# Sharing SBUF-operand work between VectorE and GpSimd by the order of the instructions, in attention followed by two feed-forward layers

## The chip, the cores and the metric

The kernel runs on one core of one Trainium2 chip. The metric is device time in microseconds (us) of one execution. TensorE is called PE here (PEld its weight loads), VectorE DVE, ScalarE ACT, GpSimd POOL, and SyncE, whose queue issues the transfers, SP.

## What is computed

Attention with 4 batches, 8 heads, 576 tokens and a head size of 64, in which only scores within `tau` of their row's maximum count. Its output, 2304 tokens of 512 numbers, goes through two feed-forward layers with a hidden size of 2048. The first uses a leaky ReLU with a slope for each hidden unit, the second x * sigmoid(x), which is Silu.

```python
scores = scale * np.matmul(q, k.transpose(0, 1, 3, 2))
thresh = np.max(scores, axis=-1, keepdims=True) - tau
scores = np.where(scores >= thresh, scores, -1000000000.0)
attn = np.exp(scores - np.max(scores, axis=-1, keepdims=True))
attn = attn / (np.sum(attn, axis=-1, keepdims=True) + 1e-09)
x = heads_side_by_side(np.matmul(attn, v))
h = x @ w_in;   g = np.maximum(h, 0.0) + alpha * np.minimum(h, 0.0);   x = g @ w_out
h = x @ w_in2;  g = h * (1.0 / (1.0 + np.exp(-h)));                    out = g @ w_out2
```

(The last three lines are put together from three functions.) The weights come as 64-bit numbers in memory; the kernel converts them itself.

## The kernel before

**Attention** works on 16 pairs of heads, each with 9 units of up to 128 rows of scores. For each of the 144 units PE multiplies into PSUM; DVE scales, copies to SBUF and takes the extreme (`maxi`, L481, `x<-s,nsc`: it reads PSUM); ACT takes the exponential (`expo`, L494); and DVE compares with the threshold and multiplies (`mask`, L507, `e<-x,m,e`: both operands in SBUF). Then come transposes, the products with v, and `evac` (L594, `X<-pv,px`) into the tiles X0, X1 and X2, each with 768 tokens.

**Each layer** goes in 12 passes: 4 groups of 512 hidden units by 3 pieces p of 768 tokens. A pass forms 7 products of the Strassen kind (`PORD`: 1, 7, 6, 2, 5, 3, 4), each of 2 x 6 matmuls, since every operand stands as a high part and a rest, and three of the four cross products are taken. `piece` makes the token side of a product in an `xs` tile: subtractions for T2, T3 and T4 into `ta` and `tb` (L342), ACT's high part (`one`, L223), and the rest `x - high` (L346), which POOL does for every other product and DVE for the others. In a layer's first group the pieces are made; they are stored, and read back for the later groups. Product sums go through `c<-c,su`, `su<-s,su` and `s<-s,su` (L854, L858, L864: one operand in PSUM) to `act`, which makes the hidden value `r` (L753 and L754 in the first layer; in the second Sigmoid, L757, and a multiplication, L758), its high part and its rest `g` (L760, 192 times). Then PE forms the output blocks y (`yblock`, L775 and L777; 8 a pass in the first layer, 6 in the second), half of them at the end of the pass, half in the next.

**Weights** are converted by `conv`, one 128x512 block at a time: 4 `wi` and 4 `wo` for each group. A block is loaded as `raw`; two ACT steps and five DVE steps (L290, L292, L294, L299 or L301, L302) make a float `cv`, with `cm` and `ce` as scratch; and a high part and a rest are written to the `wi` or `wo` tile (for `wi` after four sums into `cs`, L314). The product `ce<-ce,cm` is done by DVE in attention (L301) and by POOL after it (L299). During attention six blocks (4 `wi`, `WOA` = 2 `wo`) and the pieces of products 1 and 7 are prepared.

**What sets the order.** All of it is issued by two planners that place steps in a model with assumed durations. `plan` (attention) has PE follow the list `ORDER`; on the other engines, of the steps that can start first, the one with the smallest priority number goes, and conversions and pieces have the last. `plan_late` (the layers) takes the step that is due first, counting back from PE's order. Each engine then runs its queue in the order that was planned and waits only for data. Every step is tied to one engine, and both planners treat DVE and POOL as engines that don't touch each other:

```python
t = max(free[e], min(ready[n] for n in able(e)))
n = min((n for n in able(e) if ready[n] <= t), key=lambda n: (ops[n][3], rank[n]))
```

Of the kernel before, what the change touches and what calls it, by code (L numbers as in the profile page):

```python
# [41 lines left out]
XO = 40  # L42
XSB = 5
WIB = 7
WOB = 8
WOA = 2
GB = 12
RSB = 3
VB = 2
RB = 2  # L50
# [37 lines left out]

def plan(ops, order, seq):
    left, ready, out, after = {}, {}, [], {}  # L90
# [5 lines left out]
    free = {e: 0.0 for e in ("PE", "DVE", "ACT", "POOL", "SP")}  # L96
    cand = {e: [] for e in free}
    rank = {n: i for i, n in enumerate(ops)}
    for n in ops:
        if not left[n]:  # L100
            cand[ops[n][0]].append(n)
# [48 lines left out]
def plan_late(ops):  # L150

    n = len(ops)
    after = [[] for _ in range(n)]
# [14 lines left out]
    free = {e: 0.0 for e in ("PE", "DVE", "ACT", "POOL", "SP")}  # L168
    cand = {e: [] for e in free}
    for i, o in enumerate(ops):  # L170
        if o[0] != "PE" and not left[i]:
            cand[o[0]].append(i)
    k, out = 0, []
    while True:
        best = None
        for e in free:
            c = ([pe[k]] if k < len(pe) and not left[pe[k]] else []) if e == "PE" else cand[e]
            if c:
                t = max(free[e], min(ready[i] for i in c))
                if best is None or t < best[0]:  # L180
                    best = (t, e, c)
# [3 lines left out]
        i = min((i for i in c if ready[i] <= t), key=lambda i: (late[i], i))  # L185
        if e == "PE":
            k += 1
        else:
            cand[e].remove(i)
        o = ops[i]  # L190
        free[e] = t + o[1]
        out.append((t, len(out), i))
        for j in after[i]:
            ready[j] = max(ready[j], t + (o[1] if e == ops[j][0] == "PE" else o[2]))
            left[j] -= 1
            if not left[j] and ops[j][0] != "PE":
                cand[ops[j][0]].append(j)
    assert len(out) == n
# [4 lines left out]
def attn_moe_moe(  # L203
# [66 lines left out]
    def conv(kind, n, r, pool):  # L270
# [7 lines left out]
        else:  # L278
# [647 lines left out]
```

## Time and profile before

| | |
|---|---|
| three runs, median | 1086.74 us (1085.68 to 1087.17) |
| the profiled execution, its own time | 1087.49 us |
| its span, first to last instruction | 1085.7 us |
| mean granted TensorE clock | 0.991 of full |
| busy: PE, DVE, ACT, POOL | 96%, 79%, 60%, 12% of the span |

The span leaves out 1.8 us that lie around the instructions. A busy share is a mean over stages with different limits, so the stretches below are read one by one. The duration of an instruction in the records runs from its start to its end, and time in which it stands still after its start is part of it.

### The profile page before, as it was taken

What the parts mean: (1) busy time and instruction counts of PE and PEld (TensorE: products, weight loads), DVE (VectorE), ACT (ScalarE), POOL (GpSimd) and SP (SyncE); (2) the same over time, 40 slices, a digit from 0 to 9 for tenths busy, and PEclk for the clock granted to TensorE, in tenths of its full rate; (3) what the DMA queues carried; (4) which work ended last, traced back from release to release, by engine and by line L of the source; (5) the groups of instructions that cost most, each with busy time, mean ns of one, the idle gap of its engine ahead of it and who ended that gap; (6) DMA issues with size and microseconds to landing.
All of it is one profiled execution on the core that took longest, in us unless ns stands there. A gap on an engine that the chain in (4) does not pass through costs nothing.

```text
span 1085.7 us, 16589 instructions
## 1 busy us (share of the span) xinstructions
PE 1045.5 (96%) x6020; PEld 887.6 (82%) x6021; DVE 856.2 (79%) x1880; ACT 650.6 (60%) x1303; POOL 126.6 (12%) x88
## 2 busy tenths in 40 slices
PE   9999999999778999999999999899999999999998
PEld 5665666566577999999999998887898888889987
DVE  7999999999589887688768787887778588655443
ACT  6889889988556675455545545666565355333320
POOL 0000000000243321001101102233111011000000
PEclk9999999999989999999999999999999999999999
DMA  3223223141354775576765665455676555555632
GB/s 106 89 75 103 84 80 103 53 150 39 145 203 195 244 253 197 185 257 242 238 215 190 213 211 203 155 214 185 232 262 230 196 191 217 174 204 204 228 130 78
DMA packets 43601, 189.30 MB, mean 174 GB/s; under 512 B 5120, under 2 KB 5504, under 8 KB 43520
## 3 DMA queue, kind: packets, MB, share of 16 engines
q1 hardware_dynamic: 43216, 187.97, 49.6%
q8 instruction: 47, 0.77, 0.3%
q10 hardware_dynamic: 304, 0.28, 0.1%
q14 instruction: 34, 0.28, 0.1%
HBM read 150.48 MB, written 37.75 MB: 173 GB/s over the span
## 4 chain that ended last, share of the span: by engine, by line
PE 67%; DVE 23%; issue 5%; POOL 2%; ACT 2%; POOLq 0%; DVEq 0%; ACTq 0%
PE s L359 20%; PE y L777 16%; PE y L775 12%; PE s L467 5%; PE t L541 4%; PE pv L575 4%; PE c L359 3%; DVE x L481 3%; DVE e L507 3%; DVE g L760 3%; POOL ce L299 2%; DVE r L754 2%; DVE r L758 1%; DVE cv L302 1%; DVE cv L292 1%
## 5 line engine op out<-in xcount | busy, mean ns | idle before, releaser
L359 PE MATMUL s<-xs,wi 128*128 128x384 f32 x1728 | 327.2, 341 | 22.2 <-DVE su L858 5.1
L359 PEld LDWEIGHTS s<-xs,wi 128*128 128x128 f32 x1728 | 304.7, 190 | 36.3 <-DVE r L758 7.8
L775 PE MATMUL y<-g,wo 128*128 128x384 f32 x1152 | 209.8, 338 | 10.0 <-ACT g L223 4.1
L775 PEld LDWEIGHTS y<-g,wo 128*128 128x128 f32 x1152 | 201.8, 190 | 14.4 <-DVE X L792 4.8
L777 PE MATMUL y<-wo,g 128*128 128x512 f32 (+1 forms) x876 | 202.0, 389 | 1.3 <-DVE X L792 0.7
L777 PEld LDWEIGHTS y<-wo,g 128*128 128x128 f32 x876 | 163.1, 189 | 34.9 <-DVE X L792 1.2
L223 ACT ACTIVATE su<-s 128x384 f32<-128x384 f32 x144 | 70.3, 489 | 111.6 <-PE s L359 110.7
L299 POOL TENSOR_TENSOR ce<-ce,cm 128x512 f32<-128x512 f32 x58 | 78.5, 1353 | 455.3 <-ACT cm L296 232.9
L223 ACT ACTIVATE g<-r 128x384 fp32r<-128x384 f32 x192 | 97.8, 523 | 36.2 <-DVE r L754 21.1
L481 DVE TENSOR_SCALAR_CACHE_REDUCE x<-s,nsc 128x576 f32<-128x576 f32 x144 | 112.5, 814 | 1.9 <-PE s L467 1.6
L760 DVE TENSOR_TENSOR g<-r,g 128x384 fp32r<-128x384 f32 x192 | 108.5, 584 | 0.0
L467 PE MATMUL s<-raw 64*128 64x288 f32 (+1 forms) x576 | 100.8, 427 | 1.0 <-DVE x L481 1.0
L507 DVE SCALAR_TENSOR_TENSOR e<-x,m,e 128x577 f32<-128x577 f32 x128 | 100.1, 811 | 1.2 <-ACT m L501 1.1
L494 ACT ACTIVATE e<-x,m 128x576 f32<-128x576 f32 x128 | 97.1, 785 | 5.0 <-DVE x L481 4.8
L792 DVE TENSOR_TENSOR X<-y,X 128x384 f32<-128x384 f32 (+1 forms) x108 | 64.5, 598 | 31.4 <-PE y L777 20.8
L467 PEld LDWEIGHTS s<-raw 64*128 64x128 f32 (+1 forms) x576 | 57.0, 186 | 39.2 <-DVE x L481 11.3
L302 DVE TENSOR_TENSOR cv<-cv,ce 128x512 f32<-128x512 f32 x64 | 48.0, 750 | 45.9 <-POOL ce L299 45.8
L541 PEld LDWEIGHTS t<-ident,e 128*128 128x128 f32 x576 | 63.1, 141 | 20.5 <-issue 8.9
L541 PE MATMUL t<-ident,e 128*128 128x128 f32 x576 | 79.6, 279 | 0.2 <-DVE e L507 0.2
L223 ACT ACTIVATE pt<-t 128x512 f32<-128x512 f32 x128 | 70.6, 605 | 14.4 <-PE t L541 14.1
L289 ACT ACTIVATE cm<-raw 128x512 f32<-128x512 f32 x64 | 43.1, 673 | 54.9 <-POOL ce L299 44.9
L854 DVE TENSOR_TENSOR c<-c,su 128x384 f32<-128x384 f32 x48 | 26.9, 563 | 58.3 <-PE c L359 57.9
(91 smaller groups left out, 1183.5 us busy)
## 6 DMA issues: line engine op xcount, KB each, us to landing
xs<-xd SPq DMA_DIRECT2D x126, 768.0 KB, 5.7
xd<-xs SPq DMA_DIRECT2D x42, 768.0 KB, 4.0
raw<-in_w1i SPq DMA_DIRECT2D x16, 512.0 KB, 4.9
raw<-in_w1o SPq DMA_DIRECT2D x16, 512.0 KB, 4.5
raw<-in_w2i SPq DMA_DIRECT2D x16, 512.0 KB, 3.8
raw<-in_w2o SPq DMA_DIRECT2D x16, 512.0 KB, 3.6
rv<-in_v SPq DMA_DIRECT2D x16, 480.0 KB, 3.5
raw<-in_q SPq DMA_DIRECT2D x15, 320.0 KB, 3.3
```

The costliest lines, as they stand in the source:

```text
L223: e.activation(out=dst, in_=src, func=AF.Copy)
L299: st.append(("POOL", 1.3, 1.45, ["cm", "ce"], ["ce"], lambda: P.tensor_tensor(out=ce, in0=ce, in1=cm, op=ALU.mult)))
L359: T.matmul(bank, WIN[halves[c] % WIB][:, x, AI[a], :], xs[:, y, c, :], start=start and k == 0, stop=stop and k == 5, skip_group_check=True,)
L467: T.matmul(SP[u + k][:, hf, :S // 2], RAW[i][p, 0, q], RAW[i][p, 1, c], start=True, stop=True)
L481: V.tensor_scalar(out=x.rearrange("p (a b) -> p a b", a=2), in0=SP[u][:, :, :S // 2], scalar1=nsc, scalar2=None, op0=ALU.mult, op1=ALU.min ...
L494: A.activation(out=ES[u], in_=xts[u % XB][:, 1:S + 1], func=AF.Exp, bias=mcol(u, 0), scale=-1.0)
L507: V.scalar_tensor_tensor(out=e, in0=x, scalar=mcol(u, 1), in1=e, op0=ALU.is_le, op1=ALU.mult, accum_out=mcol(u, 2))
L541: T.transpose(TP[n][:, c * 128:(c + 1) * 128], EP[i, t // 2][:, o:o + 128], ident)
L760: add(*dve_step(HN, [rk, gk], [gk], lambda: V.tensor_tensor(out=gt[:, 1], in0=rt, in1=gt[:, 0].bitcast(F32), op=ALU.subtract)))
L775: T.matmul(yt[:, :HN], WOUT[wos[f]][:, a, i * 128:(i + 1) * 128], GT[gs[f, k]][:, c], **kw)
L777: T.matmul(yt[:, :wd], GT[gs[f, k]][:, a, i * 128:(i + 1) * 128], WOUT[wos[f]][:, c, hs], **kw)
L792: add(*dve_step(n, [yk] + cell, cell, lambda: V.tensor_tensor(out=dst, in0=src, in1=dst, op=ALU.add)))
```

## The change

1. Three kinds of step are told apart: `DVE` (at most one operand in SBUF), `DVE+` (DVE alone, but with both operands in SBUF, or the integer steps of a conversion), and `BOTH` (both operands in SBUF; DVE or POOL may run it). Both planners keep a time until which the operands' way is taken (`port`): a `DVE+` or `BOTH` step on DVE starts after POOL's last step, and one on POOL after DVE's last such step. POOL is taken to need twice DVE's time. In `plan` POOL takes whatever it can start earlier; in `plan_late` only what has over `POOL_SLACK` = 4 us until it is due.
2. Attention prepares two more `wo` blocks (`WOA` 2 to 4) near its end, and the piece of product 6 (T2, `XA` = 3); pieces may begin 60 instead of 40 units before the end. Only one `raw` buffer is there during attention, and the tile for PE's idle matmuls is laid over `cs`.
3. The first pass leaves all its 8 output blocks to the second, which does four of them after its fifth product, where one was done before. So four blocks (48 matmuls) move behind products of the second pass on PE.
4. The second layer's Sigmoid and multiplication become one ACT step, Silu.

Instruction counts by the order: POOL's two-operand steps go from 81 to 155 (72 of them `g`); DVE loses 96 multiplications; PE and ACT keep theirs.

```diff
-XO = 40
+XO = 60
 XSB = 5
 WIB = 7
 WOB = 8
-WOA = 2
+WOA = 4
+XA = 3
 GB = 12
 RSB = 3
 VB = 2
+POOL_RATE = 2.0
+POOL_SLACK = 4.0
+POOL_TAIL = 0.2
...
+    def est(e, n):
+        t = max(free[e], ready[n])
+        if e == "DVE" and ops[n][0] != "DVE":
+            t = max(t, port["POOL"])
+        if e == "POOL" and ops[n][0] == "BOTH":
+            t = max(t, port["DVE"])
+            if free["DVE"] > t + POOL_TAIL:
+                t = max(t, free["DVE"])
+        return t
...
+        e = min((x for x in free if able(x)), key=lambda x: min(est(x, n) for n in able(x)))
+        t = min(est(e, n) for n in able(e))
+        n = min((n for n in able(e) if est(e, n) <= t), key=lambda n: (ops[n][3], rank[n]))
...
+        if eng == "BOTH":
+            cand["DVE" if e == "POOL" else "POOL"].remove(n)
+            if e == "POOL":
+                dur = dur * POOL_RATE + 0.15
+                fin = dur + 0.15
+        free[e] = t + dur
+        if eng in HOME:
+            port[e] = t + dur
...
+    def est(e, i):
+        t = max(free[e], ready[i])
+        if e == "DVE" and ops[i][0] != "DVE":
+            t = max(t, port["POOL"])
+        if e == "POOL":
+            t = max(t, port["DVE"])
+        return t
...
+            if e == "POOL":
+                c = [i for i in c if late[i] + shift > max(free["DVE"], ready[i]) + POOL_SLACK]
...
+            shift = max(shift, t - late[i])
         else:
             cand[e].remove(i)
-        o = ops[i]
-        free[e] = t + o[1]
-        out.append((t, len(out), i))
+            if o[0] == "BOTH":
+                cand["DVE" if e == "POOL" else "POOL"].remove(i)
+        if e == "POOL":
+            dur = dur * POOL_RATE + 0.15
+            fin = dur + 0.15
+        free[e] = t + dur
+        if e == "POOL" or e == "DVE" and o[0] != "DVE":
+            port[e] = t + dur
...
-    slots(big, XS, range(2), [128, 2, 2, HN], "xs")
+    slots(big, XS, range(XA), [128, 2, 2, HN], "xs")
...
-    raws = [big.tile([128, 512, 2], I32, name=f"raw{i}") for i in range(2)]
+    raws = {0: big.tile([128, 512, 2], I32, name="raw0")}
...
+    def dve_step(n, reads, writes, fn, us=None, port=False):
+        us = us or v_us(n)
+        return ("DVE+" if port else "DVE", us, us + 0.12, reads, writes, fn)
+
+    def both_step(n, reads, writes, fn):
+
+        return ("BOTH", v_us(n), v_us(n) + 0.12, reads, writes, fn)
...
+            both_step(512, ["cm", "ce"], ["ce"], lambda e: e.tensor_tensor(out=ce, in0=ce, in1=cm, op=ALU.mult)),
+            both_step(512, ["cv", "ce"], ["cv"], lambda e: e.tensor_tensor(out=cv, in0=cv, in1=ce, op=ALU.add)),
         ]
-        if pool:
-            st.append(("POOL", 1.3, 1.45, ["cm", "ce"], ["ce"], lambda: P.tensor_tensor(out=ce, in0=ce, in1=cm, op=ALU.mult)))
-        else:
-            st.append(dve_step(512, ["cm", "ce"], ["ce"], lambda: V.tensor_tensor(out=ce, in0=ce, in1=cm, op=ALU.mult)))
-        st.append(dve_step(512, ["cv", "ce"], ["cv"], lambda: V.tensor_tensor(out=cv, in0=cv, in1=ce, op=ALU.add)))
...
-            st.append(dve_step(512, ["cv", key], [key], lambda: V.tensor_tensor(
+            st.append(both_step(512, ["cv", key], [key], lambda e: e.tensor_tensor(
...
-            st.append(dve_step(2 * HN, x[1] + y[1], o[1], lambda o=o, x=x, y=y: V.tensor_tensor(
+        for o, x, y in pre if part & 1 else []:
+            st.append(both_step(2 * HN, x[1] + y[1], o[1], lambda e, o=o, x=x, y=y: e.tensor_tensor(
...
-        lo = lambda e: e.tensor_tensor(out=x[:, 1], in0=src[0], in1=x[:, 0].bitcast(F32), op=ALU.subtract)
-        if pool:
-            st.append(("POOL", 2.0, 2.15, src[1] + [key], [key], lambda: lo(P)))
-        else:
-            st.append(dve_step(2 * HN, src[1] + [key], [key], lambda: lo(V)))
+        st.append(both_step(2 * HN, src[1] + [key], [key], lambda e: e.tensor_tensor(
+            out=x[:, 1], in0=src[0], in1=x[:, 0].bitcast(F32), op=ALU.subtract)))
...
-        zero = qp.tile([128, 512], BF16, tag="zero", name="zero")
+        zero = cs.bitcast(BF16)[:, :512]
...
-            op(("mask", u), "DVE", 0.74, 2, [("exp", u), ("thr", i, g)], lambda u=u: mask(u), 0.9)
+            op(("mask", u), "DVE+", 0.74, 2, [("exp", u), ("thr", i, g)], lambda u=u: mask(u), 0.9)
...
-            wdone.append(chain(("w", j), conv("wi" if j < 4 else "wo", j if j < 4 else j - 4, j % 2, False), after))
+            wdone.append(chain(("w", j), conv("wi" if j < 4 else "wo", j if j < 4 else j - 4, 0), after))
         src = [qk(NU - XO)] + [x for i in range(2 * HP) for x in (("evac", i), ("evac8", i))]
-        xdone = [chain(("xa", n), piece(0, PROD[n][1], k), src) for k, n in enumerate(PORD[:2])]
+        xdone = [chain(("xa", n), piece(0, PROD[n][1], k), src) for k, n in enumerate(PORD[:XA])]
...
-                add(*act_step(HN, [key], [rk], lambda: A.activation(out=rt, in_=src(), func=AF.Sigmoid)))
-                add(*dve_step(HN, [rk, key], [rk], lambda: V.tensor_tensor(out=rt, in0=src(), in1=rt, op=ALU.mult)))
+                add(*act_step(HN, [key], [rk], lambda: A.activation(out=rt, in_=src(), func=AF.Silu)))
             add(*act_step(HN, [rk], [gk], lambda: one(A, gt[:, 0], rt)))
-            add(*dve_step(HN, [rk, gk], [gk], lambda: V.tensor_tensor(
+            add(*both_step(HN, [rk, gk], [gk], lambda e: e.tensor_tensor(
...
-                    if vi or qi > 1:
-                        addall(piece(p, b, slot, pool=qi % 2 == 0))
+                    if vi or qi >= XA:
+                        addall(piece(p, b, slot))
...
-                    yblock(*pend.pop(0))
+                    for _ in range(NC if vi == 1 else 1):
+                        yblock(*pend.pop(0))
...
-            for x in pend + blocks[0]:
-                yblock(*x)
-            pend = blocks[1]
+            if vi:
+                for x in pend + blocks[0]:
+                    yblock(*x)
+                pend = blocks[1]
+            else:
+                pend = blocks[0] + blocks[1]
```

**POOL's first two-operand steps.** Before, they come after attention (`xs4`, `xs2` are pieces of the first pass):

```order
masks.py:199 AFFINE_SELECT ident_61<-ident_61 128x128
L624 TENSOR_SCALAR neg_67<-alp_66 128x16
L346 TENSOR_TENSOR xs4_3068<-tb_84,xs4_3068 128x768
L346 TENSOR_TENSOR xs2_3066<-ta_83,xs2_3066 128x768
L299 TENSOR_TENSOR ce_89<-ce_89,cm_87 128x512
```

With the change the steps below stand in the place of attention, and three more (`ce`, `wo0`, `ce`) behind them; `wi0` to `wi2` are weight blocks, `xs2` the piece of product 6:

```order
L693 TENSOR_SCALAR neg_67<-alp_66 128x16
L370 TENSOR_TENSOR ce_91<-ce_91,cm_89 128x512
L371 TENSOR_TENSOR cv_90<-cv_90,ce_91 128x512
L389 TENSOR_TENSOR wi0_75<-cv_90,wi0_75 128x384
L389 TENSOR_TENSOR wi1_76<-cv_90,wi1_76 128x384
L389 TENSOR_TENSOR wi1_76<-cs_92,wi1_76 128x512
L370 TENSOR_TENSOR ce_91<-ce_91,cm_89 128x512
L389 TENSOR_TENSOR wi2_77<-cv_90,wi2_77 128x384
L389 TENSOR_TENSOR wi2_77<-cs_92,wi2_77 128x512
L412 TENSOR_TENSOR ta_86<-X0_72,tb_87 128x768
L418 TENSOR_TENSOR xs2_85<-ta_86,xs2_85 128x768
L370 TENSOR_TENSOR ce_91<-ce_91,cm_89 128x512
```

Conversion steps and the piece of product 6 have moved from DVE, or from after attention, to POOL during it.

**DVE where attention ends.** Before, the last mask (`z`), the last `X2<-pv`, then the pieces of the first pass and a conversion:

```order
L507 SCALAR_TENSOR_TENSOR z_122,m_2774<-x3_134,m_2774,z_122 128x577
L516 RECIPROCAL m_2774<-m_2774 128x1
L602 TENSOR_TENSOR X2_74<-t_2996,q8_3005 64x64 x2
L594 TENSOR_TENSOR X2_74<-pv_3007,px_2929 128x512
L346 TENSOR_TENSOR xs3_3067<-X0_72,xs3_3067 128x768
L342 TENSOR_TENSOR ta_83<-X0_72,tb_84 128x768
L342 TENSOR_TENSOR tb_84<-X1_73 128x768
L290 TENSOR_SCALAR cm_87<-cm_87 128x512
L292 SCALAR_TENSOR_TENSOR cv_88<-raw0_85,cm_87 128x512
L342 TENSOR_TENSOR ta_83<-X0_72,ta_83 128x768
L294 TENSOR_SCALAR ce_89<-cv_88 128x512
```

With the change:

```order
L671 TENSOR_TENSOR X2_74<-t_3016,q8_3026 64x64 x2
L363 TENSOR_SCALAR cm_89<-cm_89 128x512
L365 SCALAR_TENSOR_TENSOR cv_90<-raw0_88,cm_89 128x512
L367 TENSOR_SCALAR ce_91<-cv_90 128x512
L370 TENSOR_TENSOR ce_91<-ce_91,cm_89 128x512
L371 TENSOR_TENSOR cv_90<-cv_90,ce_91 128x512
L663 TENSOR_TENSOR X2_74<-pv_3028,px_2937 128x512
L375 TENSOR_TENSOR wo3_82<-cv_90,wo3_82 128x512
L418 TENSOR_TENSOR xs3_3091<-X0_72,xs3_3091 128x768
L418 TENSOR_TENSOR xs4_3092<-tb_87,xs4_3092 128x768
L412 TENSOR_TENSOR tb_87<-X1_73 128x768
L927 TENSOR_TENSOR c0_3125<-c0_3125,su0_3116 128x384
```

The steps of the last `wo` conversion (`wo3`) now stand ahead of and around the last `X2<-pv`, those of `wo2` right before them, and `ta<-X0,tb` is gone from here.

## Rows read from the trace of the kernel before

**Rows 1.** The page, part 1: busy us, share of the span and instructions of each engine.

```profile
PE 1045.5 (96%) x6020; PEld 887.6 (82%) x6021; DVE 856.2 (79%) x1880; ACT 650.6 (60%) x1303; POOL 126.6 (12%) x88
```

**Rows 2.** Stretches: length, then busy us (count) of PE, PEld, DVE, ACT, POOL; granted clock.

```profile
12.00:271.60 259.60, 257.46 (x1874) 160.60 (x1872) 257.21 (x724) 226.72 (x474) 0.00 (x0) 1.00 0.26 84
271.60:279.30 7.70, 7.63 (x58) 3.78 (x58) 0.61 (x3) 4.14 (x9) 0.00 (x0) 1.00 0.01 2
279.30:399.60 120.30, 103.28 (x537) 97.85 (x536) 101.60 (x168) 76.39 (x149) 39.73 (x22) 0.94 0.59 215
399.60:656.00 256.40, 253.32 (x1438) 249.95 (x1437) 196.38 (x405) 131.31 (x258) 29.93 (x23) 0.99 0.64 220
656.00:796.00 140.00, 130.11 (x662) 117.89 (x661) 116.12 (x205) 87.57 (x166) 38.61 (x23) 0.99 0.54 195
796.00:1060.40 264.40, 260.88 (x1302) 233.88 (x1301) 170.30 (x335) 117.35 (x239) 17.39 (x13) 1.00 0.58 203
```

**Rows 3.** Chain that ended last, in order of time: start, us, what and how many.

```profile
490.09 6.24 PE s L359 x36
838.67 13.64 PE y L777 x60
```

**Rows 4.** Stretches, for matmuls that write y alone (length, PE busy us and count, clock).

```profile
656.00:796.00 140.00, 69.83 (x324) 0.99 0.54 195
796.00:1060.40 264.40, 136.95 (x589) 1.00 0.58 203
```

**Rows 5.** Timeline of POOL and DVE, first passes: start, us, engine, line, operation, idle before.

```profile
284.86 1.80 POOL L346 TENSOR_TENSOR xs<-ta,xs 128x768 fp32r<-128x768 f32 x1
284.94 2.54 DVE L342 TENSOR_TENSOR tb<-X 128x768 f32<-128x768 f32 x1 [3.06 <-POOL xs L346]
287.41 0.41 DVE L290 TENSOR_SCALAR cm<-cm 128x512 int32<-128x512 int32 x1
287.86 0.69 DVE L292 SCALAR_TENSOR_TENSOR cv<-raw,cm 128x512 int32<-128x512 int32 x1
288.46 0.95 DVE L342 TENSOR_TENSOR ta<-X,ta 128x768 f32<-128x768 f32 x1
...
364.68 1.95 DVE L294 TENSOR_SCALAR ce<-cv 128x512 int32<-128x512 int32 x1
...
400.12 1.71 DVE L319 TENSOR_TENSOR wi<-cs,wi 128x512 fp32r<-128x512 f32 x1
```

**Rows 6.** Timeline of POOL and DVE between the two layers.

```profile
664.77 2.24 POOL L346 TENSOR_TENSOR xs<-ta,xs 128x768 fp32r<-128x768 f32 x1 [6.84 <-ACT xs L223]
665.22 0.56 DVE L864 TENSOR_TENSOR s<-s,su 128x384 f32<-128x384 f32 x1
665.68 2.21 DVE L760 TENSOR_TENSOR g<-r,g 128x384 fp32r<-128x384 f32 x2
...
764.05 1.30 POOL L299 TENSOR_TENSOR ce<-ce,cm 128x512 f32<-128x512 f32 x1 [3.36 <-DVE ce L294]
764.76 1.47 DVE L760 TENSOR_TENSOR g<-r,g 128x384 fp32r<-128x384 f32 x2
```

**Rows 7.** Groups by line and shape: busy us, mean ns of one, idle before.

```profile
L481 DVE TENSOR_SCALAR_CACHE_REDUCE x<-s,nsc 128x576 f32<-128x576 f32 x144 | 112.5, 814 | 1.9 <-PE s L467 1.6
L507 DVE SCALAR_TENSOR_TENSOR e<-x,m,e 128x577 f32<-128x577 f32 x128 | 100.1, 811 | 1.2 <-ACT m L501 1.1
L758 DVE TENSOR_TENSOR r<-s,r 128x384 f32<-128x384 f32 x48 | 26.0, 553 | 9.7 <-PE s L359 7.1 <-ACT r L757 2.2
L757 ACT ACTIVATE r<-s 128x384 f32<-128x384 f32 x48 | 23.3, 489 | 19.2 <-DVE s L864 10.0 <-PE s L359 7.1 <-DVE g L760 0.9
```

**Rows 8.** Timeline of PE: two of its waits in the first passes.

```profile
286.72 0.61 PE L359 MATMUL s<-xs,wi 128*128 128x384 f32 x2 [2.11 <-POOL xs L346]
...
307.50 0.44 PE L775 MATMUL y<-g,wo 128*128 128x384 f32 x1 [4.07 <-ACT g L223]
```

**Rows 9.** PE's waits from 796 to 1060: us in total, times, longest us.

```profile
PE s L359 <- DVE r L758: 3.5, 8, 1.2
```

More of the change, by code (lines that the diff above doesn't have):

```diff
@@ L96, in plan, with enter @@
     free = {e: 0.0 for e in ("PE", "DVE", "ACT", "POOL", "SP")}
+    port = {"DVE": 0.0, "POOL": 0.0}
     cand = {e: [] for e in free}
     rank = {n: i for i, n in enumerate(ops)}
+    def enter(n):
+        eng = ops[n][0]
+        cand[HOME.get(eng, eng)].append(n)
+        if eng == "BOTH":
+            cand["POOL"].append(n)
     for n in ops:
         if not left[n]:
-            cand[ops[n][0]].append(n)
+            enter(n)
     last, pe = "", 0
@@ L152, in plan_late @@
     n = len(ops)
+    home = [{"DVE+": "DVE", "BOTH": "DVE"}.get(o[0], o[0]) for o in ops]
     after = [[] for _ in range(n)]
@@ L168, in plan_late, with enter @@
     free = {e: 0.0 for e in ("PE", "DVE", "ACT", "POOL", "SP")}
+    port = {"DVE": 0.0, "POOL": 0.0}
     cand = {e: [] for e in free}
+    def enter(i):
+        cand[home[i]].append(i)
+        if ops[i][0] == "BOTH":
+            cand["POOL"].append(i)
     for i, o in enumerate(ops):
         if o[0] != "PE" and not left[i]:
-            cand[o[0]].append(i)
+            enter(i)
+    def est(e, i):
[5 more added lines that the diff above has]
+        return t
     k, out = 0, []
+    shift = 0.0
     while True:
@@ L260, in act_step @@
     def act_step(n, reads, writes, fn):
-        return ("ACT", a_us(n), a_us(n) + 0.22, reads, writes, fn)
-    def dve_step(n, reads, writes, fn, us=None):
-        return ("DVE", us or v_us(n), (us or v_us(n)) + 0.18, reads, writes, fn)
+        return ("ACT", a_us(n), a_us(n) + 0.14, reads, writes, fn)
+    def dve_step(n, reads, writes, fn, us=None, port=False):
[3 more added lines that the diff above has]
+        return ("BOTH", v_us(n), v_us(n) + 0.12, reads, writes, fn)
     def dma_step(n_bytes, reads, writes, fn):
@@ L314, in conv @@
             st.append(dve_step(128, ["cv", "cs"], ["cs"], lambda i=i, x=x, y=y, op=op: V.tensor_tensor(
-                out=s4[:, i], in0=x, in1=y, op=op)))
+                out=s4[:, i], in0=x, in1=y, op=op), port=True))
         for a, z, x, k in ((0, 3, v4[:, 0:3], "cv"), (3, 7, s4, "cs")):
@@ L327, in cells, with piece @@
         return [2 * e + k - 1 for e in (2 * j - 2, 2 * j - 1)]
-    def piece(p, name, slot, pool=False):
+    def piece(p, name, slot, part=3):
         def q(j, k):
@@ L703, in attn_moe_moe @@
             order["z", k] = ("z", k - 1)
+        pick = {"DVE": V, "POOL": P}
+        for n, o in ops.items():
+            if o[0] == "BOTH":
+                ops[n] = (*o[:5], lambda e, fn=o[5]: fn(pick[e]))
         for fn in plan(ops, order, [step(*x) for x in line] + [None]):
@@ L714, in attn_moe_moe @@
         GT, R, SU = {}, {}, {}
+        raws[1] = pool.tile([128, 512, 2], I32, name="raw1")
         slots(pool, GT, range(GB), [128, 2, HN], "g")
@@ L877, in attn_moe_moe @@
         done, ends = plan_late(ops)
-        for _, _, i in done:
-            ops[i][4]()
+        pick = {"DVE": V, "POOL": P}
+        for _, _, i, e in done:
+            if ops[i][0] == "BOTH":
+                ops[i][4](pick[e])
+            else:
+                ops[i][4]()
 def kernel(**inputs):
```

52 lines of the change are left out of this document (28 added, 24 removed).

## The prediction

> **What bounds the kernel now.** I began with the page's busy shares [rows 1]: TensorE (PE) is busy for 96% of the span, so whatever can be won lies in the few places where it is not, and where its granted clock falls. The table of stretches [rows 2] shows these places. From 12 to 271.6 us (attention) VectorE (DVE) is busy 257.21 of 259.60 us: it sets the end there. After that PE should set it, so I count matmuls. One product matmul takes 6.24/36 = 0.1733 us, and so does one of a first-layer output block, which has the same shape; one of a second-layer block takes 13.64/60 = 0.2273 us [rows 3]. Count times price, taken from each stretch, gives what PE lost there:
> - 279.3 to 399.6 (the first passes): 537 x 0.1733 = 93.1 of 120.3 us, so 27.2 lost. PE stood idle for 17.0 of them, and at a mean granted clock of 0.94 about an eighth of the stretch ran at 1.2 instead of 2.4 GHz, which costs PE up to 7.2.
> - 399.6 to 656: 1438 x 0.1733 = 249.2 of 256.4, so 7.2 lost.
> - 656 to 796 (into the second layer): 662 matmuls, of which 324 write y [rows 4]; 48 of these are the last blocks of the first layer. (338 + 48) x 0.1733 + 276 x 0.2273 = 129.6 of 140.0, so 10.4 lost.
> - 796 to 1060.4: 713 x 0.1733 + 589 x 0.2273 = 257.4 of 264.4, so 7.0 lost.
>
> Together 51.8 us. The timelines of DVE and GpSimd (POOL) show one cause. In [rows 5] `tb<-X` takes 2.54 us where `ta<-X,ta`, of the same shape, takes 0.95: it began while POOL ran a subtraction from 284.86 on. In [rows 6] a pair of `g<-r,g`, begun at 665.68 beside POOL, lasts 2.21 us, while `s<-s,su`, as wide, keeps its 0.56 under the same POOL instruction; it reads one operand from PSUM. So DVE stands still when both its operands are in SBUF and POOL is at work. The Trainium skill (SBUF — State Buffer, section "Who interferes with whom") says that the loser of this shared port pair "fully blocks"; the trace agrees, 2.54 for 0.95. From each such instruction I subtracted the duration of the undisturbed row of its shape: 11 cost 14.5 us between 284.94 and 364.68 (the first and the last are in [rows 5]), one cost 1.0 at 400.1, and 13 cost 12.5 between 665.68 and 764.76 [rows 6]. That is 28.0 us under POOL's 126.6 [rows 1], or 0.22 us for each us of POOL.
>
> **The change part by part.** The sum is made against the profiled execution, 1087.49 us (span 1085.7 and 1.8 around it), which is 0.07% above the median of the runs shown.
>
> *A, attention.* By the order, POOL, idle there before, takes 13 instructions: 8 of 512 columns, 3 of 384, 2 of 768. The 512s and 384s leave DVE: 8 x 0.69 + 3 x 0.55 = 7.2 us [rows 5, 7]; one `ta<-X,ta` (0.95) comes in. DVE saves 6.2. POOL's prices are 1.30 at 512 [rows 6] and 1.80 at 768 [rows 5], so 1.05 at 384 on a line through these: 8 x 1.30 + 3 x 1.05 + 2 x 1.80 = 17.1 us. If none of it blocks a mask (`e<-x,m,e`, 0.81 us, both operands in SBUF [rows 7]), A is -6.2; if all does, +10.9. At 0.22 it is 3.7: I take -2.5. The step beside it, `x<-s` (0.81 [rows 7]), reads PSUM. The two added conversions fall into DVE's idle tail, where it works 0.61 of 7.70 us [rows 2]: 2 x (2 x 0.41 + 4 x 0.69) = 7.2 us [rows 5]. They share one raw buffer, and the last `X<-pv` is queued between them; if that cover is short, the first pieces of the first layer come up to 3 us later, which the range takes in.
>
> *B, first passes.* T2's operand is now made in attention, so PE's wait of 2.11 on POOL's `xs` goes [rows 8]. The first pass's four output blocks move behind products of the second pass, so the wait of 4.07 on `g` goes too [rows 8]; the products now stand in front of them and wait for their own pieces. DVE's load between the ends hardly falls (two conversions fewer, but `ce` comes back from POOL), so what it gains is the 14.5 us of blocking. Half of the 7.2 at the low clock I count as won, 3.6, since the clock falls where PE stands idle. That leaves 27.2 - 6.2 - 7.2 = 13.8 lost to chains behind DVE; I count a third, 4.6, for the blocking that goes, and 1.5 back for POOL's slower results: 6.2 + 3.6 + 4.6 - 1.5 = -13 rounded. Ends: -2 (T2 alone) and -22.
>
> *C, 399.6 to 656.* One block of 1.0 and the clock of 0.99, up to 1.3 us; chains are the rest of the 7.2. -2.5, between 0 and -5.
>
> *D, into the second layer.* The 12.5 us of blocking stand in front of 10.4 lost by PE, but part of it is chains that stay: -6, between -1 and -9.
>
> *E, Silu.* 96 multiplications of 0.55 (53 us [rows 7]) leave DVE, which is busy 170 of 264 us from 796 on [rows 2], so only waits count: PE waited 3.5 us in 8 places for exactly this step [rows 9], and its PSUM bank now comes free without it. -3, between -1 and -5. Silu has no row; Sigmoid takes 0.489 [rows 7], and I take the same. Twice that would add 47 us to ACT, which is busy 117 of the 264, and is hidden but for some of the chain; nothing if it is shorter. The saving in D is inside the -6. From 1060.4 on nothing changes.
>
> Sum: -2.5 - 13 - 2.5 - 6 - 3 = -27, so **1060.5 us**.
>
> **Rivals.**
> - *POOL's turns in attention all cost DVE.* Condition: a mask stands at DVE's head whenever POOL starts. For it: DVE has 1% of room. Against it: two `x<-s` often stand together in the order. A is +10.9: 1060.5 + 13.4 = 1073.9. By the skill's rule named above, with a full block for each instruction, this is the case. Chance 0.13.
> - *The turns don't hold in the layers.* The order rests on assumed durations. Once the engines slip, POOL's 142 instructions there (83 x 1.05 + 43 x 1.30 + 16 x 1.80 = 172 us) block at the old 0.22: 38 us, more than before. Then only A, 2.1 + 1.4 in B and E remain: 1087.5 - 9 = 1078.5. Chance 0.16.
> - *Slower: POOL's queue becomes the late one.* 72 of 192 `g<-r,g` go to POOL at 1.05 for 0.55, queued behind conversion steps that wait for ACT or a landing. An output block that finds its `g` late makes PE wait, as the 4.07 us shows. From 27/24 = 1.1 us in each of the 24 passes it decides; at 1.5 it gives 1060.5 + 36 = 1096.5. Against it: the planner gives POOL only steps with 4 us to spare. Chance 0.06.
> - *All of it comes.* PE loses only 15 of the 51.8 and attention gives the full 6.2: 1087.5 - 36.8 - 6.2 = 1044.5. Against it: chains stay, and DVE's load in B stays. Chance 0.12.
> - That Silu would swap tables with Copy at each use, and so not be one step, is excluded: the order has one table load in the second layer, as before.
>
> **How the numbers follow.** The forecast has 0.53; its own range is 1051 (A at -6.2, B at -19) to 1070 (A at 0, B at -6). The range over the cases, 1045 to 1080, leaves out the slower case and the far ends of the second and fourth, some 0.16. A difference under 0.2% (2.2 us) can't be told from none. Faster by more than that is everything but the slower case and the far end of the second: 0.89; same 0.04; slower 0.07.
>
> **What would show it.** Attention: POOL rows of about 1.3 us beside `x<-s`, masks still near 0.81, PE's first product of T2 without a wait. First passes: the summed blocking of DVE well under 14.5 us and PE's loss in the matching stretch near 14. Second layer: no DVE row at twice its own length between 656 and 790, and the waits on the multiplication gone. I am wrong if masks average over 0.9 us (first rival), if DVE's two-operand rows are stretched by over 20 us in sum (second), or if PE's waits name POOL's `g` (third).

## The result and the profile after

The changed kernel takes **1067.28 us** (median of 4 runs, 1067.2 to 1068.2), the kernel before 1086.67 beside it: a ratio of 0.9825, 95% interval 0.9808 to 0.9842. It is 19.4 us faster; forecast were 27. The profiled execution took 1068.2 us (span 1066.4).

The first part of the page after (columns as in [rows 1]):

```profile
PE 1038.0 (97%) x6021; PEld 885.5 (83%) x6021; DVE 807.5 (76%) x1710; ACT 653.5 (61%) x1303; POOL 190.5 (18%) x162
```

The stretches after, cut at the same points of the work as [rows 2], and the y matmuls of the last two as in [rows 4]:

```profile
12.00:275.30 263.30, 261.56 (x1888) 163.53 (x1888) 256.05 (x720) 230.10 (x480) 17.19 (x13) 1.00 0.26 83
275.30:283.00 7.70, 7.55 (x60) 3.59 (x58) 5.14 (x11) 4.85 (x10) 0.00 (x0) 1.00 0.20 70
283.00:392.60 109.60, 99.53 (x532) 95.64 (x531) 96.18 (x162) 75.72 (x144) 21.55 (x16) 0.94 0.63 229
392.60:653.70 261.10, 251.77 (x1437) 248.23 (x1437) 193.15 (x359) 131.26 (x258) 78.09 (x69) 1.00 0.61 216
653.70:783.10 129.40, 126.47 (x661) 116.82 (x660) 112.04 (x191) 88.96 (x168) 35.77 (x24) 1.00 0.59 214
783.10:1041.40 258.30, 258.30 (x1303) 234.21 (x1302) 132.05 (x233) 116.45 (x235) 36.85 (x34) 1.00 0.59 206
```

```profile
653.70:783.10 129.40, 67.86 (x324) 1.00 0.59 214
783.10:1041.40 258.30, 136.87 (x589) 1.00 0.59 206
```

| term | length before, after | forecast | measured | lost by PE before, after |
|---|---|---|---|---|
| A, to the end of attention | 279.3, 283.0 | -2.5 | **+3.7** | |
| B, first passes | 120.3, 109.6 | -13 | -10.7 | 27.2, 17.4 |
| C, rest of layer 1 | 256.4, 261.1 | -2.5 | **+4.7** | 7.2, 12.1 |
| D, into layer 2 | 140.0, 129.4 | -6 | -10.6 | 10.4, 0 |
| E, layer 2 | 264.4, 258.3 | -3 | -6.1 | 7.0, 0.7 |
| the last 25 us | 25.3, 25.0 | 0 | -0.3 | |

The sum is -19.3, the difference of the spans. "Lost" is worked out with the prices of [rows 3], as before: 109.6 - 532 x 0.1733 = 17.4, and so on. Two terms have the wrong sign. **C** shows in the waits of PE from 400 to 650 us:

```profile
PE s L428 <- DVE r L828: 8.5, 7, 1.5
PE s L428 <- ACT r L827: 0.8, 1, 0.8
```

L828 makes `r` in the first layer. One such place, on the timelines of DVE and POOL together (sorted by start; two DVE steps are left out at the dots), and then of PE:

```profile
525.94 1.99 POOL L833 TENSOR_TENSOR g<-r,g 128x384 fp32r<-128x384 f32 x2 [0.48 <-ACT g L291]
...
527.16 1.71 DVE L828 SCALAR_TENSOR_TENSOR r<-r,neg,su 128x384 f32<-128x384 f32 x2
...
528.98 1.02 POOL L833 TENSOR_TENSOR g<-r,g 128x384 fp32r<-128x384 f32 x1 [1.05 <-ACT g L291]
529.46 0.95 DVE L833 TENSOR_TENSOR g<-r,g 128x384 fp32r<-128x384 f32 x1
531.29 1.14 DVE L828 SCALAR_TENSOR_TENSOR r<-r,neg,s 128x384 f32<-128x384 f32 x2 [0.88 <-PE s L428]
```

```profile
527.87 3.31 PE L428 MATMUL s<-xs,wi 128*128 128x384 f32 x18
532.48 1.32 PE L428 MATMUL s<-xs,wi 128*128 128x384 f32 x6 [1.30 <-DVE r L828]
```

The 18 matmuls that end at 531.18 are product 3 and the first half of product 4. Only then does DVE, which had stood idle for 0.88 us, start on the two `r<-r,neg,s` of product 3, and the second half of product 4 starts (532.48) when the second of them has ended. By the order of the program the first `r<-r,neg,s` stands behind the first half of product 4, and the second in front of its second half. These steps share no data: the results of products 3 and 4 lie in two banks, A and B, of one tile `s` for each half, and the built program makes a step on one bank wait for the step ahead of it on the other. The planner keeps A and B apart, so it doesn't know these waits. Seven of the 12 passes of the first layer have this order, six of them between the 4th and the 12th. PE waits 1.30 us in each and 1.50 in one; these six waits are 8.0 of the 8.5 us above.

The instructions of L828 by operand (count, then min, median and max in ns):

```profile
L828 DVE SCALAR_TENSOR_TENSOR r<-r,neg,s x48: 599/607/616, 299.3 to 667.1; 128x384 f32<-128x384 f32 x48
L828 DVE SCALAR_TENSOR_TENSOR r<-r,neg,c x24: 603/606/617, 290.9 to 656.9; 128x384 f32<-128x384 f32 x24
L828 DVE SCALAR_TENSOR_TENSOR r<-r,neg,su x24: 605/1018/2284, 295.5 to 660.7; 128x384 f32<-128x384 f32 x24
```

One form of the step reads `su`, so both its operands lie in SBUF, and half of its 24 take 1.0 us or more. The planner has it in the class `DVE`, though it belongs in `DVE+`: it puts POOL's `g` over it, and the stops of this form sum to 9.1 us. But all 12 waits of PE for L828 end with a `r<-r,neg,s`, the form that is never stopped.

**A**: the masks rose from 811 to 825 ns ([rows 7] before), the extreme steps kept their 814, and DVE now waits for PE's scores (first the two groups on the page, then DVE's waits from 12 to 272 us):

```profile
L550 DVE TENSOR_SCALAR_CACHE_REDUCE x<-s,nsc 128x576 f32<-128x576 f32 x144 | 112.5, 814 | 6.4 <-PE s L536 6.2
...
L576 DVE SCALAR_TENSOR_TENSOR e<-x,m,e 128x577 f32<-128x577 f32 x128 | 102.1, 825 | 1.5 <-ACT m L570 1.1
```

```profile
DVE x L550 <- PE s L536: 4.2, 10, 0.9
DVE e L576 <- ACT m L570: 0.8, 1, 0.8
```

**B**: both waits of [rows 8] are gone; three others stand on PE's timeline, and one long dip of the granted clock (1.2 instead of 2.4 GHz; the row of that stretch is the second fence) begins after the first of them, in which PE had stood for 2.54 us:

```profile
299.92 2.20 PE L428 MATMUL s<-xs,wi 128*128 128x384 f32 x6 [2.54 <-DVE r L828]
304.16 2.29 PE L428 MATMUL s<-xs,wi 128*128 128x384 f32 x6 [2.04 <-DVE r L828]
307.62 7.21 PE L428 MATMUL s<-xs,wi 128*128 128x384 f32 x24 [1.17 <-DVE r L828]
```

```profile
300.05:313.70 13.65, 10.44 (x31) 9.42 (x32) 11.60 (x14) 5.89 (x11) 4.53 (x3) 0.50 0.55 202
```

Summed as in the prediction, DVE's stops beside POOL are 42 us, where they were 28: 2.0 in A (before none), 8.5 in B (14.5), 15.3 in C (1.0), 11.5 in D (12.5) and 4.6 in E (none).

### The profile page after: what moved, and what is told of

It is laid out like the page before. It is cut to its first block, busy times and chain, and to the rows that moved or that the text cites. A ratio compares the mean times of both kernels' runs of the same rounds, so it can differ in the third digit from the quotient of the medians.

```text
span 1066.4 us, 16597 instructions
## 1 busy us (share of the span) xinstructions
PE 1038.0 (97%) x6021; PEld 885.5 (83%) x6021; DVE 807.5 (76%) x1710; ACT 653.5 (61%) x1303; POOL 190.5 (18%) x162
## 4 chain that ended last, share of the span: by engine, by line
PE 85%; DVE 9%; ACT 3%; issue 2%; DVEq 0%; ACTq 0%
PE s L428 25%; PE y L850 18%; PE y L848 15%; PE s L536 8%; PE t L610 6%; PE pv L644 6%; PE c L428 4%; DVE r L828 2%; DVE x L550 1%; DVE e L576 1%; PE t L651 1%; DVE ta L412 1%; PE t L616 1%; DVE g L833 1%; ACT g L291 1%
## 5 line engine op out<-in xcount | busy, mean ns | idle before, releaser
L428 PE MATMUL s<-xs,wi 128*128 128x384 f32 x1728 | 324.3, 340 | 21.6 <-DVE r L828 16.5
L848 PE MATMUL y<-g,wo 128*128 128x384 f32 x1152 | 204.5, 334 | 0.7 <-DVE X L865 0.7
L291 ACT ACTIVATE su<-s 128x384 f32<-128x384 f32 x144 | 70.5, 489 | 129.4 <-PE s L428 127.9
L833 POOL TENSOR_TENSOR g<-r,g 128x384 fp32r<-128x384 f32 x72 | 74.9, 1047 | 333.2 <-ACT g L291 321.9
L550 DVE TENSOR_SCALAR_CACHE_REDUCE x<-s,nsc 128x576 f32<-128x576 f32 x144 | 112.5, 814 | 6.4 <-PE s L536 6.2
L833 DVE TENSOR_TENSOR g<-r,g 128x384 fp32r<-128x384 f32 x120 | 77.2, 651 | 22.1 <-ACT g L291 19.9
L369 ACT ACTIVATE cm<-raw 128x512 f32<-128x512 uint16 x64 | 43.2, 676 | 47.3 <-DVE cv L365 46.4
```

Source lines behind the costliest of these rows:

```text
L291: e.activation(out=dst, in_=src, func=AF.Copy)
L428: T.matmul(bank, WIN[halves[c] % WIB][:, x, AI[a], :], xs[:, y, c, :], start=start and k == 0, stop=stop and k == 5, skip_group_check=True,)
L550: V.tensor_scalar(out=x.rearrange("p (a b) -> p a b", a=2), in0=SP[u][:, :, :S // 2], scalar1=nsc, scalar2=None, op0=ALU.mult, op1=ALU.min ...
L833: add(*both_step(HN, [rk, gk], [gk], lambda e: e.tensor_tensor(out=gt[:, 1], in0=rt, in1=gt[:, 0].bitcast(F32), op=ALU.subtract)))
L848: T.matmul(yt[:, :HN], WOUT[wos[f]][:, a, i * 128:(i + 1) * 128], GT[gs[f, k]][:, c], **kw)
```

## The experiments

All are compared by the same marks of the work: the last weight load of `pv` (attention ends), the first `c<-c,su` of the 4th, 12th and 16th pass, and PE's end. Total is the median; the kernel before, run beside each set, gave 1085.6 to 1086.8.

| kernel | attention ends | to pass 4 | 4 to 12 | 12 to 16 | 16 to end | total |
|---|---|---|---|---|---|---|
| before | 278.4 | 120.2 | 257.3 | 139.9 | 286.5 | 1086.7 |
| the change | 282.0 | 109.5 | 262.0 | 129.4 | 280.4 | 1067.3 |
| 1, class of L828 mended | 281.7 | 107.6 | 253.7 | 130.0 | 280.4 | 1058.1 |
| 2, layer 1's g on DVE | 282.1 | 106.8 | 255.7 | 130.0 | 280.4 | 1060.4 |
| 3, no POOL in attention | 281.4 | 109.7 | 262.6 | 129.3 | 280.4 | 1068.2 |
| 4, before + Silu | 279.1 | 118.3 | 255.7 | 136.7 | 280.5 | 1076.0 |
| 5, preparation undone | 285.0 | 120.1 | 261.3 | 129.3 | 280.4 | 1081.6 |
| 6, block move undone | 282.1 | 110.2 | 262.2 | 129.3 | 280.4 | 1068.8 |
| 7, turns alone | 285.5 | 112.5 | 260.7 | 132.4 | 284.4 | 1081.1 |
| 8, turns alone, mended | 285.9 | 110.5 | 254.2 | 133.9 | 284.2 | 1072.4 |
| 9, POOL idle | 281.5 | 108.1 | 254.3 | 128.8 | 280.6 | 1058.6 |
| 10, 1 and 3 | 281.6 | 107.8 | 253.6 | 130.1 | 280.4 | 1058.7 |
| 11, 1 with 8 us to spare | 281.6 | 107.1 | 255.1 | 130.3 | 280.5 | 1057.5 |
| 12, 1 and 2 | 281.9 | 108.3 | 254.4 | 129.5 | 280.4 | 1058.4 |

**1. The class mended.**

```diff
-                    out=rt, in0=rt, scalar=neg[:, f:f + 1], in1=src(), op0=ALU.mult, op1=ALU.add), 0.53))
+                    out=rt, in0=rt, scalar=neg[:, f:f + 1], in1=src(), op0=ALU.mult, op1=ALU.add), 0.53, port=key[0] == "su"))
```

> Theory (the planner's classes have a hole): `r<-r,neg,su` reads both operands from SBUF, yet it is classed as a step that needs no turn, so POOL's g stops it, PE waits for it, and passes of the first layer take 32.8 us instead of 31.5. With that step classed as one that needs its turn, the stretch from the 4th to the 12th pass (262.0 us, before 257.3) falls to 255 to 258, the waits of PE on that step (16.5 us in the page of the changed kernel) fall under 6, and the total to 1058 to 1063 us. Rival (POOL's g are simply late, whatever the class): the stretch stays at 260 to 263 and the total within 2 us of 1067.3. Other rival (the new turns push steps aside that are due as soon): the stretch gets no shorter and the total goes above 1069.

1058.1 us, ratio to before 0.9741 (0.9725 to 0.9757). The step and PE's waits from 400 to 650 in this run:

```profile
L828 DVE SCALAR_TENSOR_TENSOR r<-r,neg,su x24: 605/613/1177, 295.3 to 661.9; 128x384 f32<-128x384 f32 x24
```

```profile
PE s L428 <- DVE r L828: 1.0, 4, 0.3
PE y L848 <- DVE X L865: 0.6, 1, 0.6
```

The time came as the theory had it: 9.2 us less, 8.3 of them between the 4th and the 12th pass, which is shorter than expected. PE's waits for L828 from attention's end on fell from 16.5 to 7.4, not under 6: the three long ones of the first passes stay. The way to it is another than the theory's. The stops fell only from 42 to 34 us, and those between 400 and 650 us from 13.5 to 10.9. What went are the waits of 1.30 us: with the mended class the planner puts out another order, in which no pass from the 4th to the 12th has the second `r<-r,neg,s` in front of the second half of product 4. Whether the right class is worth anything beyond that other order is not shown: no run changes the order alone.

**2. The first layer's g on DVE.**

```diff
+            if m == 0:
+                add("DVE+", *st, lambda: fn(V))
+            else:
+                add(eng, *st, fn)
```

> All g of the first layer stay on DVE (POOL keeps the second layer's and the conversions). If POOL's g are what costs the steady passes, by stopping the unmarked step or by coming late, the stretch from the 4th to the 12th pass falls from 262.0 to about 257 (as before the change) or a little below, and the total to 1061 to 1064 us. If DVE's load is the cause (DVE gets some 45 x 0.55 = 25 us back over twelve passes), the stretch stays above 260 and the total within 3 us of 1067.3. Against the run in which only the class of the step is mended: if that one gives the same or less time, POOL's g itself is harmless.

1060.4 us, ratio 0.9763 (0.9748 to 0.9777). Without POOL's `g` the passes are short too, though DVE does more: DVE's load was not the cause. The order around product 4 is another one here too, with no wait of 1.30 us between the 4th and the 12th pass, so this run doesn't tell the stops from the order.

**3. Attention without POOL.**

```diff
-                ops[n] = (*o[:5], lambda e, fn=o[5]: fn(pick[e]))
+                ops[n] = ("DVE+", *o[1:5], lambda fn=o[5]: fn(V))
```

> The steps prepared in attention are the same, but DVE does all of them; POOL does none until the layers. Theory (POOL's turns cost attention, since the planner puts other steps of DVE into its gaps, where they wait for PE's scores): DVE does some 17 steps or 8 us more, yet its idle time in attention falls from 7 us to about 3, attention ends within 2 us of the changed kernel's 282.0, and the total is 1065 to 1071. Rival (POOL's turns are worth what they take from DVE, and the 3.65 us that attention grew come from the start and the added conversions): attention ends 5 to 9 us later than 282.0, total 1072 to 1077. Whether the 1.1 us at the start belong to the change: the first extreme step starts at 7.1 again if they do, at about 6.0 if they are chance.

1068.2 us, ratio 0.9836 (0.9822 to 0.9851). Counted from the first extreme step, attention takes 274.9 us; with POOL 275.0; before 272.4. DVE's stretch from 12 to 272 us, here and in the changed kernel:

```profile
12.00:272.00 260.00, 257.85 (x1866) 160.50 (x1863) 257.32 (x722) 226.07 (x474) 0.00 (x0) 1.00 0.26 83
```

```profile
12.00:272.00 260.00, 258.26 (x1866) 161.03 (x1867) 252.87 (x711) 227.64 (x475) 17.19 (x13) 1.00 0.26 85
```

POOL's turns take 4.5 us off DVE there, and DVE idles 4.5 us more: it waits 4.2 us for PE's scores with them, 1.2 without. They are worth nothing here. The second part of the change (the added preparation, with one `raw` buffer) is in both runs; by elimination it costs attention the 2.5, for no run has it out while POOL idles there. The first extreme step starts between 5.97 and 7.10 us in the fourteen profiles, at 5.97 in run 5, which starts with the same code: I take A's other 1.1 us to be chance.

**4. Silu alone**, on the kernel before.

```diff
-                add(*act_step(HN, [key], [rk], lambda: A.activation(out=rt, in_=src(), func=AF.Sigmoid)))
-                add(*dve_step(HN, [rk, key], [rk], lambda: V.tensor_tensor(out=rt, in0=src(), in1=rt, op=ALU.mult)))
+                add(*act_step(HN, [key], [rk], lambda: A.activation(out=rt, in_=src(), func=AF.Silu)))
```

> The kernel before with the fourth part of the change alone: Sigmoid and multiplication become one Silu. By my prediction the stretch from the 16th pass on shortens by 3 us and the one before by 2 or 3, total 1080 to 1082 us. By the trace of the changed kernel, in which the stretch from the 16th pass on lost 6.2 us and has no wait of PE at all, Silu alone brings 6 to 10, total 1077 to 1081. If the gain there came from POOL's turns instead, under 3 us, total above 1084.

1076.0 us, ratio 0.9907 (0.9892 to 0.9921): about 10 of the 19.4 us. From the 16th pass on it gives all that the whole change gives (280.5 for 280.4), and PE is busy throughout:

```profile
789.90:1048.00 258.10, 258.10 (x1300) 233.92 (x1300) 137.82 (x257) 117.70 (x237) 17.53 (x13) 1.00 0.60 205
```

Up to 695 us the layers run in the order of the kernel before, and yet the stretches to the 4th and to the 12th pass are 1.9 and 1.6 us shorter here. By so much a stretch differs from one execution to another; differences below that in the table say nothing.

**5. The preparation undone.**

```diff
-XO = 60
+XO = 40
-WOA = 4
+WOA = 2
-XA = 3
+XA = 2
```

> The changed kernel with the second part undone: two output-weight blocks and the pieces of products 1 and 7 are prepared in attention, as before the change. Counted from the first extreme step, attention took 272.4 us before the change and 275.0 with it, with or without POOL's turns. Theory (the added preparation makes the 2.6 us): attention takes 272 to 273 again, and the first passes pay 4 to 8 us for what was prepared (T2's piece and two conversions), total 1069 to 1074. Rival (the turns and the new places of steps cost attention, the preparation lies in idle time): attention stays near 275, total 1071 to 1076. Third (the preparation buys nothing, since the first passes wait elsewhere): total 1064 to 1067.

1081.6 us, ratio 0.9959 (0.9945 to 0.9974), outside every expectation. The first passes lose 10.6: the moved blocks now wait for a weight block (first row below, PE's waits from 285 to 405). And attention gets longer, to 279.0 from the first extreme step. POOL's steps stop four masks here, three in the changed kernel; two of the four, one behind the other (DVE, then POOL):

```profile
PE y L848 <- ACT wo L291: 6.8, 1, 6.8
PE s L428 <- DVE r L828: 3.8, 3, 2.0
```

```profile
214.14 1.66 DVE L576 SCALAR_TENSOR_TENSOR e<-x,m,e 128x577 f32<-128x577 f32 x1
215.73 0.08 DVE L576 DVE_READ_ACCUMULATOR e<-x,m,e 128x1 f32 x1
215.73 2.36 DVE L576 SCALAR_TENSOR_TENSOR e<-x,m,e 128x577 f32<-128x577 f32 x1
```

```profile
213.91 1.28 POOL L375 TENSOR_TENSOR wo<-cv,wo 128x512 fp32r<-128x512 f32 x1 [34.54 <-ACT wo L291]
215.14 2.33 POOL L412 TENSOR_TENSOR ta<-X 128x768 f32<-128x768 f32 x1
```

The four masks lose 4.1 us over 0.81 each, the three of the changed kernel 1.6: that is 2.5 of the 4.1 us by which this attention is longer than the changed kernel's. So the first rival's price is real where its condition is met; what the rest is isn't shown.

**6. The move of the four blocks undone.**

```diff
-                    for _ in range(NC if vi == 1 else 1):
-                        yblock(*pend.pop(0))
+                    yblock(*pend.pop(0))
...
-            if vi:
-                for x in pend + blocks[0]:
-                    yblock(*x)
-                pend = blocks[1]
-            else:
-                pend = blocks[0] + blocks[1]
+            for x in pend + blocks[0]:
+                yblock(*x)
+            pend = blocks[1]
```

> The changed kernel with the third part undone: the first pass's first four output blocks stand at its end again. Theory (their move saves the wait of 4.1 us for g and part of what follows): that wait is back, the stretch from the end of attention to the 4th pass's sum (109.5 us) grows by 3 to 6, total 1070 to 1073. Rival (the move only shifts the wait: with it PE waits for r in the second pass and runs 13.7 us at half the clock, which costs as much): within 2 us of 1067.3, and the long stretch at half clock between 300 and 314 breaks up into short ones, as before the change.

1068.8 us, ratio 0.9842 (0.9826 to 0.9859): the move is worth some 1.6 us, at overlapping intervals. A wait for `g` is back, longer than before the change, and the three waits for `r` are gone:

```profile
305.23 0.69 PE L848 MATMUL y<-g,wo 128*128 128x384 f32 x1 [7.46 <-ACT g L291]
```

The move trades one wait for others, as the rival had it; the dip stays one, 10.2 us long.

**7 and 8. The turns alone**, without preparation, move and Silu; in 8 with the mended class. The edits are those of 5 and 6 and the reverse of 4.

> The kernel before with the first part of the change alone, the turns of DVE and POOL: preparation, output blocks and Sigmoid as before. If the parts add up: the changed kernel's 1067.3, plus 9.6 for Silu (its size alone on the kernel before), plus 3 to 6 for each of the other two, 1083 to 1089, so that the turns as the planner has them bring nothing. If the turns are what brought the gain of the first passes and of the stretch into the second layer, 1074 to 1080.

> The same with the class of `r<-r,neg,su` mended. The mending brought 9.2 us in the whole change; if the hole in the classes is what takes the worth of the turns away, it brings 7 to 11 here too, 1074 to 1080, with the stretch from the 4th to the 12th pass at 253 to 256 us. If it brings under 4, the 9.2 hung on the other parts.

1081.1 us, ratio 0.9954 (0.9939 to 0.9969), and 1072.4, ratio 0.9877 (0.9862 to 0.9892). As built, the turns bring some 5 us to the kernel before; the mending adds 8.7. They win 8 to 10 us in the first passes and 6 to 7.5 into the second layer, where the old fixed shares collided, and lose 7 of it in attention, where POOL's steps stop the same four masks as in run 5. Run 7 has the waits of 1.30 us in the same passes as the change, run 8 has none. The mending of run 8 is not whole: the second layer's `r<-su,r`, which is there without Silu and has both operands in SBUF, is still in the class `DVE`, and takes up to 1198 ns, median 552.

**9. POOL idle.** All that DVE or POOL may do goes to DVE.

```diff
-        return ("BOTH", v_us(n), v_us(n) + 0.12, reads, writes, fn)
+        return ("DVE+", v_us(n), v_us(n) + 0.12, reads, writes, lambda: fn(V))
```

> The changed kernel with every step that DVE or POOL may run given to DVE; POOL idles. DVE has some 155 steps (about 85 us) more and is never stopped (42 us of stops in the changed kernel). Theory (in the first layer the turns cost more than they take off DVE, since a stopped step stands in a chain that PE waits for): the stretch from the 4th to the 12th pass takes 254 to 258 us as against 262.0, the last eight passes and Silu's gain stay (280 to 281 us), the first passes lose 2 to 8; total 1062 to 1070, within 5 us of the changed kernel. Rival (POOL's share is needed, DVE becomes the bound of the first layer): DVE over 97% busy there, the stretch above 264, total above 1073. Other side: below 1060, so that POOL's turns as the planner has them do nothing but harm.

1058.6 us, ratio 0.974 (0.9727 to 0.9754): as fast as the mended turns, 8.7 us faster than the change. The page's busy line, and the stretch from 400 to 650:

```profile
PE 1037.7 (98%) x6020; PEld 883.7 (84%) x6021; DVE 841.5 (80%) x1865; ACT 653.3 (62%) x1303; POOL 0.9 (0%) x7
```

```profile
400.00:650.00 250.00, 248.80 (x1418) 244.95 (x1417) 206.66 (x424) 129.67 (x253) 0.00 (x0) 1.00 0.63 221
```

DVE does 155 instructions more than in the changed kernel and is busy only 34 us longer, for the 42 us of stops are gone. With Silu it has the room, and POOL isn't needed; no run leaves POOL idle without Silu. The waits of 1.30 us are gone here too. In the pass that is shown above for the changed kernel, products 3 and 4 run through on PE (24 matmuls), and each `r<-r,neg,s` stands behind its half of product 4:

```profile
521.69 4.32 PE L428 MATMUL s<-xs,wi 128*128 128x384 f32 x24
```

```profile
525.08 0.61 DVE L828 SCALAR_TENSOR_TENSOR r<-r,neg,s 128x384 f32<-128x384 f32 x1 [1.25 <-PE s L428]
...
526.12 0.61 DVE L828 SCALAR_TENSOR_TENSOR r<-r,neg,s 128x384 f32<-128x384 f32 x1
```

Between 400 and 650 us PE waits 1.1 us in all here, with no stop of DVE, and 1.6 in run 1, with 10.9 us of stops.

**10 to 12. What is left.** Run 10 joins the edits of 1 and 3, run 12 those of 1 and 2; run 11 adds to 1:

```diff
-POOL_SLACK = 4.0
+POOL_SLACK = 8.0
```

> Both findings together: the class of `r<-r,neg,su` mended, and attention without POOL. In attention POOL's turns were worth 0.1 us by the one comparison, so this should be the mended kernel's 1058.1 within 2 us. If the turns in attention help only when the layers are in order, above 1060; if they hurt, below 1056.

> The mended kernel with 8 instead of 4 us to spare for POOL in the layers, by which POOL takes 99 steps there instead of 126. Theory (what is left of the loss in the first layer, 5.7 us above eight passes at 31.0, is stops of DVE by POOL): stops fall from about 28 to 20 us in sum and the total to 1054 to 1057. Rival (what is left are chains and DVE's load): 1057 to 1060.

> The mended kernel with the g of the first layer on DVE alone. Against the run with the same g but the class unmended (1060.4) it shows whether the class matters once POOL has no g there: 1060 within 1.5 us if g was all that met `r<-r,neg,su`, 1056 to 1058 if conversions and pieces on POOL met it too. If it beats the mended kernel's 1058.1, POOL's g in the first layer are a loss even with the right classes.

1058.7 us, ratio 0.9742 (0.9729 to 0.9755); 1057.5, 0.9729 (0.9716 to 0.9743); 1058.4, 0.9736 (0.9723 to 0.9749). With run 9 and run 1 these can't be told apart. Run 11 doesn't speak for its theory: the stops fell from 34 only to 32 us. Run 12 lies 2 us below run 2 at overlapping intervals, so whether the class matters without POOL's `g` stays open.

## Why the prediction was right, and where not

The sign and the range held, by errors that offset each other. The blocking of DVE that B and D were to win back did not go: of their 27.0 us 20.0 are still there, and C has 15.3. So that the total came so near is in part luck.

- **A failed.** The step was "DVE saves 6.2", reduced to -2.5. Run 3: POOL's turns save nothing, since the order that fills their gaps waits for PE's scores. The second part of the change costs 2.5, where I had counted its work into DVE's idle tail; 1.1 I put down to the chance of the start.
- **B was mis-sized by 2.3.** T2's wait went. Of the clock I counted 3.6 as won: the mean granted clock is 0.94 as before, four dips of 3.4 us having become one of 13.65. The blocking fell by 6 us, not by 14.5. The 4.1 for the blocks is some 1.6 (run 6). What is larger than I thought is the preparation: without it the moved blocks wait 6.8 us (run 5). That and the move hang together; I priced them apart.
- **C failed, and it is the main error.** The step was "chains are the rest", -2.5, with no loss in the range: I let the chains stand as they were, though the change hands the planner a new order. In that order PE's product 4 and DVE's `r<-r,neg,s` wait for each other by turns, 8.0 us in six passes. Runs 1, 2 and 8 to 12, whose order has no such wait there, take 253.6 to 255.7 us for the 262.0. I also took the planner's classes as they are described and didn't look at which operands L828 is called with; the rule that I had read in [rows 6] says that `r<-r,neg,su` is stopped. It is, but the waits of 1.30 us don't hang on that: in each of the seven, DVE stood idle for PE just before. Why the planner with the wrong class puts out this order is open.
- **D and E were too small.** In both PE's loss is nearly all gone, and I had left a part of it to "chains that stay". Silu alone takes 6.0 from E and 3.2 from D, the turns alone 7.5 from D. In D that was not by the blocking, as I had it: 11.5 of its 12.5 us are still there. In E I counted only the waits that name the multiplication [rows 9]; the rest of the 7.0 went with it. Silu takes 492 ns (median) where Sigmoid took 489 [rows 7], as assumed, and costs ACT nothing.
- **The rivals.** The second had its condition met, stops of about 40 us in the layers, over its 20; but not its price, 1078.5: most stops stood where PE had other work. Run 1 keeps 34 us of them and is as fast as run 9, which has none. The third is not seen: PE waited for POOL's `g` nowhere. Three of 128 masks were stopped, and a mean of 825 ns denies the first in this kernel; run 5 shows it for four masks. The rule on the shared pair (the Trainium skill, SBUF — State Buffer, "Who interferes with whom") names two SBUF inputs as the condition. L828 agrees with it form by form, at most 617 ns with an operand in PSUM and up to 2284 with both in SBUF.

What bounds the kernel now: the first passes still lose some 15 us in the best runs, with the waits of 2.5 and 2.0 us for `r` and the dip in the clock. Run 6 only trades these waits for one of 7.5 us for `g`; what would take them away is open. No run gives A and B tiles of their own, or leaves POOL idle in the kernel before.

## What to carry to other kernels

Before work is shared with an engine that stops the first one, ask whether the first one needs help: with POOL idle this kernel was as fast as with the best turns. If turns are planned, sort every call of a helper by where its operands lie, and then look in the trace for instructions of one form whose median and minimum differ. Price a stop by the engine that waits behind it, not by its length: run 1 with 34 us of stops was as fast as run 9 with none. And where a wait names a helper's line, look which call of it ended the wait and what that call had waited for itself. Here it was the form that is never stopped, in an order in which two engines wait for each other over one tile.

## What the chip showed that was not expected

- The stop works both ways: in run 5 POOL's `ta<-X` took 2.33 us beside the two masks shown there; `ta<-X,tb`, of the same shape, took 1.85 to 1.86 in that run.
- A step with a single operand in SBUF can be stopped too: the integer shift `cm<-cm` (L363) takes 407 ns at least and up to 1245 in the changed kernel, as the planner's class for it assumes (10 of the 11 that meet a POOL step take over 900 ns, the other 53 at most 430); `su<-s,su`, with one operand in PSUM, never more than 559.

```profile
L363 DVE TENSOR_SCALAR cm<-cm x64: 407/426/1245, 46.7 to 907.7; 128x512 int32<-128x512 int32 x64
```

```profile
L931 DVE TENSOR_TENSOR su<-s,su x48: 543/557/559, 292.7 to 1035.0; 128x384 f32<-128x384 f32 x48
```
